# Queries of batch 0 in two token halves, transposed on TensorE, the second half inside the first dense layer

## The chip, the cores and the metric

The kernel runs on one core of one Trainium2 chip. The metric is the device time of one execution in microseconds (us); less is better. The engines are named as in the profile: PE is TensorE's matmul side, PEld its weight load, DVE is VectorE, ACT is ScalarE, POOL is GpSimd and SP is SyncE, which here only issues DMAs.

## The reference

Two layers follow each other. The first is attention within blocks, after a learnt soft sorting of the blocks (4 batches, 8 heads, 768 tokens of 64 elements, 8 blocks of 96 tokens):

```python
P = sort_net                          # (4, 8, 8, 8)
for _ in range(5):
    P = P - np.max(P, axis=-1, keepdims=True)
    P = np.exp(P)
    P = P / (np.sum(P, axis=-1, keepdims=True) + 1e-09)
    P = P / (np.sum(P, axis=-2, keepdims=True) + 1e-09)
k_sorted = np.einsum('bhij,bhjcd->bhicd', P, k_b)      # v likewise
scores = scale * np.matmul(q_b, k_sb.transpose(0, 1, 2, 4, 3))
attn = softmax(scores)
out = np.matmul(attn, v_sb)
```

The second is a dense layer with 3072 tokens, 512 model and 2048 hidden elements:

```python
h = x @ w_in
r = np.maximum(h, 0.0)
g = s * (r * r) + b
return g @ w_out
```

Inputs and output are float32; inside, the kernel works in bfloat16 with float32 sums.

## The kernel before, in words

**Tiling.** A batch has two halves of 384 tokens (TG = 384, four blocks each). A half is one tile of the dense layer; there are eight, t = 0 to 7. The order of all work is written out by hand: every engine runs its instructions in the order of the source, and the lists of "slots" say after which piece of a dense layer a piece of attention of the next batch is issued.

**Opening.** SP loads the sorting logits (L74) and v of batch 0 in four quarters (v0f, L78). POOL loads q and k of batch 0 in three parts each (L112, L113), makes the identity matrix and two helpers (L117 to L124), and in load_w (L129) loads w_in in sixteen pieces and w_out in four. PE runs 30 filler matmuls on zeros (warm, L175). The loop at L176 normalises the sorting matrix five times: one exp on ACT and six or seven small operations on DVE per round. From round 1 on, ACT copies one quarter of v into the layout that sorting needs (permute, L179) behind each exp. 

**Batch 0.** build_pd (L199) turns the matrix into pd, the moving operand that sorts keys and values. qk_piece (L227) multiplies a third of the queries with a 0/1 matrix (qid) or a third of the keys with pd: 32 matmuls of 64 columns into one PSUM tile, then a copy (evac, L219) by ACT ("A") or DVE ("D"). v_piece (L244) does a quarter of the values in the same way. The queries go first (L409 to L411), then two v pieces, three k pieces, two v pieces. s_piece (L257) makes the scores of one pair of heads (hp) for a half: 8 matmuls, one exp on ACT. p_piece (L287) multiplies with the values: 8 matmuls, a reciprocal and a product x on DVE (L303, L304). t_piece (L309) transposes x of two head pairs on PE and copies them to xt. L409 to L435 do this for half 0 and the first two score pieces of half 1.

**Buffers.** PSUM has two pools: psa with three buffers of two banks (all pieces, scores, products and first-layer outputs) and psb with two buffers of one bank (fillers, pd, transposes, second-layer outputs, and the scores of s_banks, L271). A tile waits until the one three (or two) before it in its pool has been read.

**Dense layer.** ffn1 (L348) makes eight pieces per tile: 8 matmuls of 384 columns (L361), ReLU on ACT (L371), square on DVE (gt, L372). With ahead=3, three pieces are begun with half of their matmuls. ffn2 (L376) makes three output rows of blocks with 16 matmuls each (L382), and store (L401) scales, adds the bias and sends out. The call at L504 puts the rest of batch 0's half 1 into the slots of tile 0's first layer: two score pieces by s_banks, four products, two transposes. make_bias (L462) sums w_out's rows for the constant b; POOL copies the result (L474).

**The next batches.** POOL loads v, k and q of batch 1 after w_out (L444), sorts v's layout in eight copies (v_sort, L449, L158), and loads batch 2. Batch 1's queries use qk_piece in slot 4 of tile 0's second layer (L492); for batches 2 and 3 the queries arrive as token rows (load_q_rows) and are transposed by DMA (q_dma, L331). halves (L487) gives the slots of the second layers: s0 for the first tile of a batch, s1 for the second.

## Time and profile before

| | |
|---|---|
| three runs | 235.73, 236.42, 236.75 us, median 236.42 |
| the profiled execution | 233.61 us, span 231.8 us |
| PE busy | 218.9 us of the span, of which fillers (L149) 10.5 |
| granted PE clock, mean | 0.993 |
| POOL's DMA queue | 12.85 MB, 38.4% of 16 engines' time |
| SP's DMA queue | 11.81 MB, 20.8% |
| sorting matrix done / pd ready | 12.01 / 13.85 us |
| first dense matmul | 28.42 us |
| tile 0's first layer done with half 1's attention | 42.29 us |
| first second-layer matmul | 55.17 us |

Durations that come up often (mean of one): first-layer group of 8 matmuls 1.30 us, ReLU 0.81, square 0.56, exp of a score piece 0.81, product x 0.69 and its reciprocal 0.20, eviction of 1024 elements 1.02 on ACT and 1.22 on DVE, 32 sorting matmuls about 0.6, POOL's copy in v_sort 0.89. A view's "idle before" names what ended an engine's wait; the chain of waits follows the work that ended last back to the start, so that each of its pieces is on the path. "issue" is time in which an engine waited for nothing that the profile shows. Times in the timeline count from the start of the span.

### The profile page before, as it was taken

To read this page: it belongs to the slowest core of one execution; us is meant where nothing else is said; L and a number is where in the kernel's file an instruction comes from. 1 tells how busy PE (TensorE), PEld (TensorE's weight loads), DVE (VectorE), ACT (ScalarE), POOL (GpSimd) and SP (SyncE) were. 2 spreads that over 40 slices of the span, in tenths; PEclk is the share of its full clock that TensorE was granted. 3 is DMA by queue.
4 is the path that set the end of the run, shared out by engine and by line. 5 is a ranking of instruction groups with operands and counts; after the bars stand their busy time and mean duration, and the time that the engine had idled before them with its cause. 6 is when DMAs were issued, how large, how long until landed. Compare 5 with 4: busy or idle time off the path is not lost.

```text
span 231.8 us, 5897 instructions
## 1 busy us (share of the span) xinstructions
PE 218.9 (94%) x2584; PEld 129.9 (56%) x2607; DVE 123.7 (53%) x236; ACT 98.3 (42%) x123; POOL 59.4 (26%) x97
## 2 busy tenths in 40 slices
PE   7885899999999999999999999999999999999994
PEld 3464556656555656566455565656455565554453
DVE  6764637499584665445355664446265763432221
ACT  4776764645212345665113435664024446560000
POOL 7538850696581894000000000000000000000000
PEclk9979999999999999999999999999999999999999
DMA  6999999959999958600111299200121452001112
GB/s 151 286 202 171 166 207 218 213 102 206 160 186 223 199 124 138 113 0 3 45 48 48 60 148 164 42 0 3 45 79 63 111 73 45 0 4 45 66 70 92
DMA packets 38826, 25.03 MB, mean 108 GB/s; under 512 B 29328, under 2 KB 33680, under 8 KB 38800
## 3 DMA queue, kind: packets, MB, share of 16 engines
q0 software_dynamic: 18896, 12.85, 38.4%
q1 hardware_dynamic: 19904, 11.81, 20.8%
q8 instruction: 20, 0.33, 0.5%
q14 instruction: 6, 0.05, 0.1%
HBM read 27.27 MB, written 6.29 MB: 145 GB/s over the span
## 4 chain that ended last, share of the span: by engine, by line
PE 87%; DMA 4%; ACT 3%; issue 2%; DVE 2%; SPq 1%
PE hps L361 35%; PE ops L382 34%; PE tv L248 4%; DMA v0f<-in_v_dram 4%; PE tp L236 4%; PE pv L298 3%; PE sc L263 3%; PE ops L395 2%; DVE x L304 1%; ACT rt L371 1%; PE tr L318 1%; ACT vp L156 1%; SPq L78 1%; DVE ks L223 1%; PE pe L201 0%
## 5 line engine op out<-in xcount | busy, mean ns | idle before, releaser
L361 PE MATMUL hps<-xt,wi 128*128 128x384 bf16 x512 | 85.9, 326 | 0.6 <-DVE x L304 0.5
L382 PE MATMUL ops<-wo,gt 128*128 128x512 bf16 x347 | 81.5, 379 | 2.2 <-issue 1.6
L371 ACT ACTIVATE rt<-hps 128x768 bf16<-128x768 f32 x64 | 51.7, 812 | 41.5 <-PE hps L361 38.8
L361 PEld LDWEIGHTS <-wi 128*128 128x128 bf16 x512 | 49.0, 98 | 32.6 <-DVE x L304 0.6
L372 DVE TENSOR_TENSOR gt<-rt 128x768 bf16<-128x768 bf16 x64 | 37.1, 583 | 44.3 <-ACT rt L371 44.2
L382 PEld LDWEIGHTS <-gt 128*128 128x128 bf16 x368 | 33.7, 98 | 37.0
L403 DVE SCALAR_TENSOR_TENSOR ot<-ops,s_bc,bias 128x512 f32<-128x512 f32 (+1 forms) x25 | 18.2, 729 | 37.4 <-PE ops L382 32.6
L268 ACT ACTIVATE at<-sc 112x768 bf16<-112x768 f32 x30 | 22.6, 810 | 31.5 <-PE sc L263 31.5
L304 DVE TENSOR_TENSOR x<-pv,rec 96x512 bf16<-96x512 f32 x32 | 22.0, 687 | 1.1
L158 POOL COPY vp<-rawv 128x384 bf16<-128x384 bf16 x24 | 20.0, 890 | 10.0 <-DMA rawv<-in_v_dram 9.9
L298 PEld LDWEIGHTS <-at 112*128 112x128 bf16 (+1 forms) x256 | 12.7, 101 | 7.5 <-ACT at L268 1.2
L223 DVE CAST vs<-tv 112x1024 bf16<-112x1024 f32 x11 | 13.2, 1221 | 5.9 <-PE tv L248 5.9
L99 POOL DMA_DIRECT2D qtok<-in_q_dram x16 | 12.4, 791 | 10.6 <-DMA rawv<-in_v_dram 7.6
L221 ACT CAST vs<-tv 112x1024 bf16<-112x1024 f32 x5 | 5.1, 1021 | 22.4 <-PE tv L248 22.4
L298 PE MATMUL pv<-vs,at 112*128 112x66 bf16 (+1 forms) x256 | 13.8, 195 | 0.3 <-ACT at L268 0.3
L248 PE MATMUL tv<-pd,vp 128*64 128x64 bf16 x512 | 10.7, 202 | 2.4 <-issue 1.3
L248 PEld LDWEIGHTS <-vp 128*64 128x64 bf16 x512 | 9.8, 118 | 5.6 <-issue 4.6
L303 DVE RECIPROCAL rec<-pv 96x8 f32<-96x8 f32 x32 | 6.4, 200 | 10.8 <-PE pv L298 10.8
L149 PE MATMUL z<-zeros 128*128 128x512 bf16 x37 | 10.5, 420 | 1.6 <-DVE zeros L103 1.2
L134 POOL DMA_DIRECT2D wi<-in_moe_w_in_dram x16 | 8.5, 536 | 6.8 <-DMA rawk<-in_k_dram 3.4
L263 PE MATMUL sc<-qt,ks 64*128 64x96 bf16 x240 | 8.1, 204 | 0.7 <-ACT vs L221 0.7
L223 DVE CAST ks<-tp 128x1024 bf16<-128x1024 f32 x7 | 8.3, 1219 | 0.5 <-PE tp L236 0.3
(69 smaller groups left out, 107.5 us busy)
## 6 DMA issues: line engine op xcount, KB each, us to landing
out_dram<-ot SPq DMA_DIRECT2D x23, 256.0 KB, 2.0
rawv<-in_v_dram POOLq DMA_DIRECT2D x3, 768.0 KB, 12.2
rawk<-in_k_dram POOLq DMA_DIRECT2D x3, 768.0 KB, 7.4
wi<-in_moe_w_in_dram POOLq DMA_DIRECT2D x16, 128.0 KB, 6.6
wo<-in_moe_w_out_dram POOLq DMA_DIRECT2D x4, 512.0 KB, 10.1
v0f<-in_v_dram SPq DMA_DIRECT2D x4, 384.0 KB, 6.6
qtok<-in_q_dram POOLq DMA_DIRECT2D x16, 96.0 KB, 11.2
rawq<-in_q_dram POOLq DMA_DIRECT2D x3, 256.0 KB, 7.0
```

Source lines behind the costliest of these rows:

```text
L158: eng.tensor_copy(out=o, in_=i)
L223: nc.vector.tensor_copy(out=out, in_=in_)
L248: nc.tensor.matmul(out=ps[z * GAP:(z + 1) * GAP, d, :], lhsT=VP[b % 2][:, d0 + d, :], rhs=PD[b][:, :, z, :], start=True, stop=True)
L263: nc.tensor.matmul(out=sc[:, e, n * BLK:(n + 1) * BLK], lhsT=KS[b % 2][pr, g0 + n].rearrange("p z c -> p (z c)"), rhs=q_of(b, pr, hp, half ...
L268: nc.scalar.activation(out=at, in_=sc[0:KR, :, 0:TG], func=AF.Exp, scale=scale)
L298: nc.tensor.matmul(out=pv[0:m, e, n * VW:(n + 1) * VW], lhsT=atf[:, c0:c0 + m], rhs=VS[b % 2][:, e * NG + g0 + n, :], start=True, stop=True)
L304: nc.vector.tensor_tensor(out=x[:, :, hp * 128:(hp + 1) * 128].rearrange("p n (e d) -> p e n d", e=2), in0=pvv[:, :, :, 0:D], in1=rec.unsq ...
L361: nc.tensor.matmul(out=H1[i][:, f, 0:TG], lhsT=wi[:, hp, fc:fc + 128], rhs=xt[:, :, hp, :], start=(hp == 0), stop=(hp == NHP - 1))
L371: nc.scalar.activation(out=rt, in_=h, func=AF.Relu)
L372: nc.vector.tensor_tensor(out=gt[:, 2 * i:2 * i + 2, :], in0=rt, in1=rt, op=ALU.mult)
L382: nc.tensor.matmul(out=ops, lhsT=gt[:, f, m * 128:(m + 1) * 128], rhs=wo[:, f, :], start=(f == 0), stop=(f == NF - 1))
L403: nc.vector.scalar_tensor_tensor(out=ot[:, ns], in0=ops, scalar=s_bc, in1=BIAS[0][:, ns], op0=ALU.mult, op1=ALU.add)
```

## The change

- **Loads.** The identity and emat are made first on POOL. q of batch 0 comes as two halves of 64 partitions (load_qh, six consecutive tokens per partition); POOL's order is: half 0 of q, k in three parts, w_in's first quarter in eight small pieces, its second quarter in four, half 1 of q, the rest of w_in, the two scalars, v of batch 1, w_out. v_sort(1) follows; the loads of k and q of batch 1 and of batch 2 come behind it.
- **Queries.** qid and the query matmuls are gone. q_trans transposes half a batch with 48 PE transposes into one psa tile; q_evac copies it to QT[b], a layout [half, head pair, 6, 64]. Half 0 of batch 0 is transposed before pd, with two ACT copies; half 1 in slot 1 of tile 0's first layer, with one DVE copy. Batch 1 uses the same in the second layers.
- **Scores.** s_piece and s_banks read the queries as 6 runs of 16 and write PSUM in that shape; the exp undoes it while reading.
- **Opening.** A dummy exp ahead of the loop; fillers of 256 columns (44 and 14) and all of one warm call in one PSUM tile; ACT copies a quarter of v in each of rounds 0 to 3 (before: 1 to 4).
- **Order.** Keys before values; the first two score pieces of half 0 by s_banks; the last two v pieces are evicted in token halves, DVE the first and ACT the second; t_piece handles one head pair; first-layer matmuls of pieces 0 and 1 (head pairs 0 and 1) are issued between the attention pieces. All four score pieces of half 1 are in tile 0's first layer.
- **Later.** v of batch 1 is sorted ahead of its keys in the second layer of tile 0 (slots 5, 7, 9, 11); pd of batches 2 and 3 is built in the first layers of tiles 2 and 4.

```diff
+    def load_qh(b, half):
+        if b not in QH:
+            QH[b] = rawp.tile([128, H, CQ, D], BF, tag="rawq", name="qh")
+        qv = q[b].rearrange("h (f p c) d -> f p h (c d)", f=2, c=CQ)
+        nc.gpsimd.dma_start(out=QH[b][half * 64:(half + 1) * 64].rearrange("p h c d -> p h (c d)"),
+                            in_=qv[half])
...
-    load("q", 0, 3)
-    load("k", 0, 3)
...
+    load_qh(0, 0)
+    load("k", 0, 3)
+    fill_vs(0)
...
+    for u in range(2):
+        for c in range(2):
+            for a in range(2):
+                load_wi(c * W8, (c + 1) * W8, slice(2 * u + a, 2 * u + a + 1))
+    for a in range(NHP):
+        load_wi(W4, 2 * W4, slice(a, a + 1))
+    load_qh(0, 1)
+    for c in range(2, 4):
+        for a in range(NHP):
+            load_wi(c * W4, (c + 1) * W4, slice(a, a + 1))
...
+    load("v", 1)
...
+    def q_trans(b, half):
...
+        tr = psa.tile([128, 2, 1024], BF, tag="a", name="tqa")
+        pr = slice(half * 64, (half + 1) * 64)
+        for a in range(NHP):
+            for c in range(CQ):
+                for e in range(2):
+                    o = (a % 2 * CQ + c) * 64
+                    nc.tensor.transpose(out=tr[e * 64:(e + 1) * 64, a // 2, o:o + 64],
+                                        in_=QH[b][pr, 2 * a + e, c, :], identity=ident[pr, pr])
+        return tr
+
+    def q_evac(b, half, us, eng, tr):
+        evac(eng, QT[b][:, half].rearrange("p (u a) c t -> p u (a c t)", u=2)[:, us],
+             tr[:, us, 0:2 * TG])
...
-    warm(30)
+    warm(44, 256)
     for it in range(5):
         nc.scalar.activation(out=sn, in_=sn, func=AF.Exp)
-        if it >= 1:
-            permute(nc.scalar, 0, v0f, slice((it - 1) * CV, it * CV))
-        if it == 2:
-            load_w()
+        if it < 4:
+            permute(nc.scalar, 0, v0f, slice(it * CV, (it + 1) * CV))
...
+    tq = q_trans(0, 0)
+    for u in range(2):
+        q_evac(0, 0, slice(u, u + 1), "A", tq)
+    warm(14, 256)
...
+                if byp:
+                    o = sc[:, e, 0:TG].rearrange("p (c t) -> p c t", c=CQ)[:, :, 16 * n:16 * n + 16]
+                    r = QT[b][pr, half, hp, :, 16 * n:16 * n + 16]
...
+        if byp:
+            nc.scalar.activation(out=at.rearrange("p e (t c) -> p e t c", c=CQ),
+                                 in_=sc[0:KR, :, 0:TG].rearrange("p e (c t) -> p e t c", c=CQ),
+                                 func=AF.Exp, scale=scale)
...
-    qk_piece("q", 0, 0, "A")
-    qk_piece("q", 0, CK, "A")
-    qk_piece("q", 0, 2 * CK, "D", first=lambda: build_pd(0))
+    build_pd(0)
     warm(3)
-    v_piece(0, 0, "A")
-    v_piece(0, CK, "D")
-    qk_piece("k", 0, 0, "A")
-    qk_piece("k", 0, CK, "D")
-    qk_piece("k", 0, 2 * CK, "A")
-    v_piece(0, 2 * CK, "D")
-    v_piece(0, 3 * CK, "A")
-    s_piece(0, 0, 0)
...
+    k_piece(0, 0, "A")
+    k_piece(0, CK, "D")
+    k_piece(0, 2 * CK, "A")
+    v_piece(0, 0, "D")
+    v_piece(0, CK, "A")
+    s_banks(0, 0, 0)
+    v2 = v_piece(0, 2 * CK, "D", 1)
+    v3 = v_piece(0, 3 * CK, "D", 1)
+    v2("A")
+    s_banks(0, 0, 1)
+    v3("A")
     warm(1)
     p_piece(0, 0, 0)
+    s_piece(0, 0, 2)
+    warm(1)
     p_piece(0, 0, 1)
+    t_piece(0, 0, 0, "A")
+    s_piece(0, 0, 3)
+    part(0, 0, (0,))
+    t_piece(0, 0, 1, "A")
     p_piece(0, 0, 2)
+    part(0, 0, (1,))
+    t_piece(0, 0, 2, "A")
     p_piece(0, 0, 3)
+    part(0, 1, (0, 1))
+    t_piece(0, 0, 3, "D")
...
-    ffn1(0, {0: [SB(2)], 1: [P(0, 1, 0)], 2: [SB(3)], 3: [P(0, 1, 1)], 4: [P(0, 1, 2)],
-             5: [P(0, 1, 3)], 6: [TP(0, 1, 0, "A")], 7: [TP(0, 1, 2, "D")]}, ahead=3)
-    ffn1(1, {1: [PDB(1)], 3: [PDB(2)], 4: [make_bias], 6: [PDB(3)]}, ahead=3)
+    ffn1(0, {1: [QF0()], 2: [SC(0, 1, 0)], 3: [SC(0, 1, 1)], 4: [P(0, 1, 0), SC(0, 1, 2)],
+             5: [P(0, 1, 1), TP(0, 1, 0, "A"), SC(0, 1, 3)],
+             6: [P(0, 1, 2), TP(0, 1, 1, "D")], 7: [P(0, 1, 3), TP(0, 1, 2, "A")]},
+         {0: 2, 1: 2})
+    v_sort(1)
+    part(1, 0, (0, 1))
+    t_piece(0, 1, 3, "D")
+    part(1, 1, (0, 1))
+    load1()
+    load2()
+    ffn1(1, {2: [PDB(1)], 5: [make_bias]}, {0: 2, 1: 2})
```

## The prediction

> **What bounds the kernel now.** I read the page from its top: engine table, slices, chain; then the timeline of the first 50 us.

> ```profile
> PE 218.9 (94%) x2584; PEld 129.9 (56%) x2607; DVE 123.7 (53%) x236; ACT 98.3 (42%) x123; POOL 59.4 (26%) x97
> ...
> PE   7885899999999999999999999999999999999994
> ...
> PEclk9979999999999999999999999999999999999999
> ```

> PE is full from the sixth slice (29 us) on. Only in the first five can time be won; what is added to PE later is paid in full, unless it fills a hole. The chain of waits tells what the opening waits for:

> ```profile
> 2.62 9.28 DMA v0f<-in_v_dram
> 11.90 0.02 issue
> 11.92 1.50 ACT vp L156
> 13.43 0.92 ACT qt L221
> 14.34 0.04 issue
> 14.38 1.98 PE tv L248 x64
> ...
> 19.81 1.34 issue
> 21.16 0.28 PE tv L248 x5
> ...
> 28.59 2.62 PE hps L361 x16
> ```

> The last quarter of v of batch 0 lands at 11.90; ScalarE rearranges it, evicts queries, and PE starts. The sorting matrix (pd, L213) is ready at 13.85 by the timeline; the first dense layer starts at 28.42. The windows give two disturbances in between: PE's granted clock is 0.50 from 15 to 17 us, and PE stands 1.34 us in the middle of one piece, where no instruction waits on another engine.

> Let P be the time when pd of batch 0 is ready, S the time from which the first dense layer can run through, E the time when tile 0's layer and the attention of tile 1 are done (42.29 before).

> **1. P moves from 13.85 to 14.5: +0.65.** Before, exp and rearranging copy are interleaved as exp0, exp1, copy0, exp2, copy1...; after, as exp0, copy0, exp1, copy1... ScalarE is in order, so the last exp now stands behind copy3, that is behind the last quarter of v. The quarters landed at 4.6, 7.4, 9.6 and 11.9 (issue plus 3.4 to 9.3 us). They should come earlier: POOL now makes ident and emat first (0.27 + 0.29 + 0.52 + 0.85 us in the trace, with gaps 2.1), so its first transfer is issued at 3.4, not 1.26, and SP's four have the DMA engines alone until about 4.7. In the first 14 us the SP queue moved 1.58 MB for 35.0% of the engines' time, 322 GB/s when alone; shared, it had about half. Alone from 3.0 to 4.7 gives 0.65 MB with the start-up; the other 0.92 MB takes 2.85 us alone, 5.4 shared: the quarters land at about 4.0, 5.5, 7.8, 10.1. A copy is 1.5, an exp 0.26, VectorE from exp to exp 1.48: copy0 4.0-5.5, exp1 5.55, copy1 to 7.35, exp2 7.4, copy2 to 9.35, exp3 9.4, copy3 10.2-11.7, exp4 11.75-12.0, matrix done 12.65 (12.01 before), P 1.84 later as before: 14.5. Bounds: if ScalarE never waits for v after 3.4, nine operations end at 10.7 and P is 13.25 (-0.6); if the quarters land as before, P is 16.2 (+2.35).

> **2. From P to S: 14.57 becomes 13.25, -1.3.** The queries' 96 matmuls and three evictions leave the front; 48 transposes (as small as L236's: 96 in 1.71, so 0.85) run at about 10 us, their two ScalarE copies (0.80 each, as xt<-tr) end about 14.1, under the wait for pd. Then the order is k, k, k, v, v, scores, v, v. With 0.6 per piece on PE, ScalarE eviction 1.02, VectorE 1.23, halves 0.6, two-bank exp 0.43 each, scores 0.35, and three buffers of pool psa: k evictions end P+1.7, 2.5, 2.8; v0 P+3.75, v1 P+4.2; first exps P+5.1; half evictions for token half 0 P+5.4; second exps P+6.5; first attention product P+6.35 (it waits for a filler that needs a bank); then per head pair 0.93 on VectorE, transposes 0.18, copies 0.43: the last xt arrives at P+12.45. The same walk through the kernel before gives 13.25 without its two disturbances, 14.57 with them, so I trust it to some tenths. Disturbances stay:

> ```profile
> PE 87%; DMA 4%; ACT 3%; issue 2%; DVE 2%; SPq 1%
> ...
> q8 instruction: 20, 0.33, 0.5%
> ```

> PE's 5191 instructions came in 20 packets of a queue of their own, some 260 each. Counted in PE's program order, the 1.34 us gap is at instruction 698, a second (0.49 at 62.69) at 1711, 1013 or nearly four packets further: PE ran out of instructions. Instruction 442, one packet earlier, ran at about 16.7, so the packet came 4.5 us later. In the new order instruction 442 is in v0 (P+2.1) and 698 in the second score group (P+5.45): the packet comes at P+6.6, and S is P+12.95. [...] For the clock I add 0.3 (half of some 0.6, since PE waits before pd as it did). Bounds: 12.45 (neither) and 14.4 (a packet in 6 us, as between 57.2 and 63.17, and the full clock loss).

> **3. Work carried over S: 0.** At S the new kernel has nine first-layer matmuls done (9 x 0.163 = 1.47) but still owes 48 transposes (0.85) and two score pieces (0.6).

> **4. The first layer of tile 0: +1.7 of waits, +0.4 of slower VectorE.** Before, three pieces were started ahead and PE idled 0.6 of 13.87. Now psa's three buffers also serve transposed queries, scores and products, in program order. Walk: ReLU 0.81, exp 0.81, gt 0.56, reciprocal and x 0.93, piece 1.30. The query copy on VectorE (1536 elements, twice xt's 0.56: 1.1) stands behind gt of piece 1 and ends S+3.9, PE would score at S+3.3: 0.6. Later pieces wait 0.2 (ReLU 4), 0.25 (x of pair 0), 0.1, 0.25 (x of pair 2), and the last transposes 0.9: x of pair 3 stands behind the gt of piece 7 on VectorE. Sum 2.3, less the 0.6 of before. And POOL's sort of v(1) moves into this stage: v(1) is now asked for ahead of wo, 4.46 MB into POOL's transfers, at 0.19 MB/us (windows 12 to 21 us) landed by about 31, sorted 31 to 38. What such a neighbour costs VectorE shows where it ran before (42.4 to 49.75):

> ```profile
> 42.99 0.69 DVE L372 TENSOR_TENSOR gt<-rt 128x768 bf16<-128x768 bf16 x1 [1.08 <-ACT rt L371]
> ...
> 45.93 2.32 DVE L372 TENSOR_TENSOR gt<-rt 128x768 bf16<-128x768 bf16 x2 [1.79 <-ACT rt L371]
> ```

> gt took 0.91 on average there against 0.56, and nobody waited for it; now x and the transposes stand behind it. Five fall under the sort, 0.35 each, 1.75, of which a quarter lies on the path: 0.4. [...] Bounds for all of 4: 0 (buffers turn round as before) and +3.5 (waits of 2.3 plus all 1.75).

> **5. Later: +0.1.** Batch 1's queries: 96 matmuls and three evictions become 96 transposes and two copies, equal on PE. K, V and Q of batch 1 now stand closer together in the second layer of tile 0 (some 700 PE instructions in 11.6 us, 4.2 per packet against 4.5 to 6 to fetch): +0.3 beside the old 0.49. The bias copies stood behind query loads that waited for DMA until 60.32, and VectorE waited 2.5 for them; POOL's next loads now follow the sort at 38, while wo still moves, where the queue ran dry before (102 GB/s in one slice): -0.2. pd of batches 2 and 3 only moves. Bounds -0.5 and +1.

> Edits at nothing: the dummy exp (the table load ended at 2.03, exp0 waits for VectorE until 2.81); SP's order is unchanged; on POOL every transfer waits for the eighth before it, as wi waited for rawq and rawk, and the weights still come in time: by P+9 = 23.5 POOL's queue has moved about 0.55 MB shared and 2.5 alone, the first layer's first pieces need 1.7. The second query half lands by about 21, is needed at 28.6. wo ends by about 42, the bias matmuls read it at about 49. Were that cover gone, PE would wait for the difference. Matmuls with rows of 16 strided elements and PSUM output of that shape are not in the trace: below, 0.043 each as L263's; above, twice that, 96 of them in the full part, +4.1. PE reads xt with gaps between its rows at 0.163 per 384 columns, the nearest row: I take 0. ScalarE's strided PSUM reads cost 1.0 ns per element in ks<-tp, as plain ones.

> **Sum:** 0.65 - 1.3 + 0 + 2.1 + 0.1 = +1.55. The profiled execution took 233.61 (span 231.8 and 1.8 around it), so 235.2; it ran below the runs shown (median 236.42), and on their scale it is **238.0**, 0.7% slower. About 0.5%, 1.2 us, is what a measurement of this kernel can tell from no change.

> **Rivals.**
> - *PE is fed in the first layer (faster).* If buffers and VectorE keep up, the waits of 4 fall to 0.5, the packet comes in time (S = P+12.45, -2.1), and P is 14.2: 0.35 - 2.1 + 0.5 = -1.25 to -2.0 with P earlier, so about 234.8. For it: ScalarE has only 10.5 us of work in a stage of 15, VectorE 9.9. Against: program order puts x behind gt. It decides when the waits of 4 are under 0.5.
> - *No change.* Only v lands early (P 13.4): 1.55 - 1.1 = +0.45, 236.9.
> - *v lands as late as before (slower still).* Half of q and k on POOL's queue still take their share, P is 16.2: 1.55 + 1.7 = +3.25, 239.7. For it: 9.28 us on the chain before. Against: POOL's 2 us later start.

> **How the numbers follow.** Forecast 0.40 (0.30 slower, 0.10 within 0.5%), fed PE 0.25, no change 0.15, late v 0.20. So faster 0.25, same 0.25, slower 0.50. The range goes from 233.5 (P -0.6, S -2.1, 4 at +0.3, later -0.5: -2.9) to 240.9 (late v, and a further 1.2 from the upper bounds of 2 and 4); strided matmuls at double cost are left out, with under 0.1. The forecast's own range is 237 to 239.2.

> **What would show it.** Step 1: landing of the last v quarter and the last exp near 10.1 and 11.75, pd near 14.5. Step 2: first hps at P+8.5 to 9, a mid-piece "issue" gap in the second score group. Step 4: hps and pv waiting on ACT and DVE between 28 and 45, 2 us or more, gt above 0.8 while POOL copies v. I am wrong if pd comes before 13.9, if PE idles under 0.8 in that stage, or if scores take over 0.5 per piece.

## The result, and the profile after

The changed kernel takes 245.66 us (median of four runs, 244.11 to 246.31), the kernel before beside it 236.18 (235.73 to 236.75): a ratio of 1.039, 95% interval 1.034 to 1.045. The forecast was 238.0 with a range up to 240.9. Ratios below leave out runs over 1.5% above the fastest of their own kernel; medians keep them.

The profiled execution took 244.11, its span 242.3 against 231.8 before, 10.5 more. By the medians it is 9.5 more: the traced execution of the kernel before took 233.61 and is faster than the four runs beside the result. On the page of the changed kernel PE's slices have holes in the second to the fifth and at the sixteenth, and the granted clock dips in the third, the fifth and the sixth:

```profile
PE 223.8 (92%) x2608; PEld 134.3 (55%) x2631; DVE 124.3 (51%) x236; ACT 100.6 (41%) x129; POOL 62.6 (26%) x99
...
PE   8487699989999997999999999999999999999994
...
PEclk9979659999999999999999999999999999999999
```

The timeline of its PE shows where the opening goes (start, length, line, operation; idle time before it in brackets):

```profile
11.70 1.05 PE L209 MATMUL tqa<-ident,qh 64*64 64x64 bf16 x48 [3.41 <-DMA qh<-in_q_dram]
12.68 3.17 PE L129 MATMUL z<-zeros 128*128 128x256 bf16 x14
15.78 0.43 PE L255 MATMUL pe<-sn,emat 32*128 32x64 f32 x2
16.14 0.82 PE L129 MATMUL z<-zeros 128*128 128x512 bf16 x2
17.56 1.71 PE L280 MATMUL tp<-pd,rawk 128*64 128x64 bf16 x96 [0.60 <-DVE pd L267]
...
22.64 0.33 PE L340 MATMUL scb<-qt,ks 64*128 64x96 bf16 x7 [0.18 <-ACT at L345]
26.04 0.61 PE L129 MATMUL z<-zeros 128*128 128x512 bf16 x1 [3.07 <-issue]
```

The sorting matrix is done at 12.24, so v is no longer what it waits for. But the matmul that begins pd (L255) runs only at 15.78: it stands behind the transposes, which wait 3.41 for the first query half, and behind 14 fillers. Then PE stands 3.07 us, to 26.04, waiting for nothing that the profile shows, with a DMA share of 1.18. Both traces have 20 packets in a queue of instructions (q8, 0.33 MB); one of them moved at 23.7 us, 2.3 before PE went on, and in the kernel before one at 18.8, 2.3 before its gap ended at 21.16. So the gap is read here as a wait for instructions. The windows (busy time by engine, then the granted clock, DMA share and GB/s) show what follows:

```profile
24.00:27.00 3.00, 0.96 (x9) 0.66 (x9) 0.00 (x0) 0.34 (x1) 1.07 (x2) 0.84 1.15 170
27.00:30.00 3.00, 2.87 (x33) 1.85 (x32) 1.78 (x4) 1.90 (x3) 2.50 (x4) 0.50 1.27 180
30.00:33.00 3.00, 2.78 (x28) 1.90 (x27) 0.89 (x2) 1.05 (x3) 2.96 (x6) 0.50 0.85 138
33.00:36.00 3.00, 2.87 (x14) 1.25 (x12) 1.25 (x3) 0.06 (x1) 1.08 (x4) 0.50 1.03 194
```

PE is nearly full from 27 to 36 us and works at half its clock, in the dense layer. Later, one wait that the kernel before did not have, and POOL's share in it:

```profile
96.48 0.82 PE L409 MATMUL hps<-xt,wi 128*128 128x384 bf16 x4 [1.61 <-DMA xt<-x]
```

```profile
76.75 0.56 POOL L93 DMA_DIRECT2D rawk<-in_k_dram  x1 [9.71 <-PE tp L280]
```

The keys of batch 1 are now sorted late in the second layer of tile 0. POOL's load of batch 3's keys needs their buffer and waits for that, so it and the loads behind it (to 90 us) move beside the DMA transpose of x, which takes 7.1 us at a DMA share of 1.79, where before it took 4.2 at 0.65 (81 to 86 us).

The checkpoints, by stage (us of the profiled executions):

| stage | before | forecast | after |
|---|---|---|---|
| pd ready | 13.85 | 14.5 | 17.5 |
| from there until the first layer runs through (S) | 14.57 | 13.25 | 17.5 |
| S to the end of that stage (E, at 42.29 before) | 13.87 | 15.97 | 17.05 |
| E to the first second-layer matmul | 12.88 | | 11.70 |
| to the first layer of tile 2 | 31.62 | | 32.73 |
| from there to the end | 145.0 | | 145.8 |

The differences are +3.65, +2.9, +3.2, -1.2, +1.1 and +0.8: 10.5. E after is the start of the last transposes, 52.05; the dense matmuls behind them start at 52.23.

### The profile page after: what moved, and what is told of

The parts are those of the page before. It is cut to its first block, busy times and chain, and to the rows that moved or that the text cites. A ratio compares the mean times of both kernels' runs of the same rounds, so it can differ in the third digit from the quotient of the medians.

```text
span 242.3 us, 5949 instructions
## 1 busy us (share of the span) xinstructions
PE 223.8 (92%) x2608; PEld 134.3 (55%) x2631; DVE 124.3 (51%) x236; ACT 100.6 (41%) x129; POOL 62.6 (26%) x99
## 4 chain that ended last, share of the span: by engine, by line
PE 83%; DMA 7%; ACT 4%; DVE 3%; issue 2%; POOL 1%; POOLq 0%
PE hps L409 34%; PE ops L433 31%; DMA qh<-in_q_dram 4%; PE tv L290 3%; PE pv L361 3%; DMA xt<-x 3%; PE sc L322 2%; PE tp L280 2%; PE z L129 2%; ACT rt L421 2%; PE ops L446 1%; PE tqa L209 1%; PE tr L378 1%; ACT vs L196 1%; DVE gt L422 1%
## 5 line engine op out<-in xcount | busy, mean ns | idle before, releaser
L409 PE MATMUL hps<-xt,wi 128*128 128x384 bf16 x512 | 88.6, 331 | 2.5 <-DMA xt<-x 1.6
L421 ACT ACTIVATE rt<-hps 128x768 bf16<-128x768 f32 x64 | 51.7, 811 | 46.3 <-PE hps L409 44.2
L422 DVE TENSOR_TENSOR gt<-rt 128x768 bf16<-128x768 bf16 x64 | 40.7, 639 | 43.9 <-ACT rt L421 43.4
L454 DVE SCALAR_TENSOR_TENSOR ot<-ops,s_bc,bias 128x512 f32<-128x512 f32 (+1 forms) x25 | 18.2, 730 | 36.3 <-PE ops L433 32.7
L361 PEld LDWEIGHTS <-at 112*128 112x128 bf16 (+1 forms) x256 | 13.9, 106 | 7.0 <-ACT at L330 0.6
L129 PE MATMUL z<-zeros 128*128 128x256 bf16 (+1 forms) x62 | 12.2, 367 | 4.3 <-issue 3.1
L196 ACT CAST vs<-tv 112x1024 bf16<-112x1024 f32 (+1 forms) x7 | 6.3, 899 | 23.2 <-PE tv L290 23.2
L326 ACT ACTIVATE at<-sc 112x768 bf16<-112x768 f32 x14 | 10.9, 809 | 10.6 <-PE sc L322 10.5
L361 PE MATMUL pv<-vs,at 112*128 112x66 bf16 (+1 forms) x256 | 14.8, 202 | 0.0
L198 DVE CAST vs<-tv 112x1024 bf16<-112x1024 f32 (+1 forms) x11 | 12.1, 1124 | 5.0 <-PE tv L290 4.9
L139 POOL DMA_DIRECT2D wi<-in_moe_w_in_dram x20 | 10.7, 552 | 8.6 <-DMA qh<-in_q_dram 5.8
L129 PEld LDWEIGHTS <-zeros 128*128 128x128 bf16 x63 | 7.6, 125 | 7.1 <-issue 3.2
L290 PEld LDWEIGHTS <-vp 128*64 128x64 bf16 x512 | 8.9, 113 | 3.0 <-issue 2.7
```

Source lines behind the costliest of these rows:

```text
L129: nc.tensor.matmul(out=z[0:m, 0:w], lhsT=zeros[:, 0:m], rhs=zeros[:, 0:w], start=True, stop=True)
L198: nc.vector.tensor_copy(out=out, in_=in_)
L290: nc.tensor.matmul(out=ps[z * GAP:(z + 1) * GAP, d, :], lhsT=VP[b % 2][:, d0 + d, :], rhs=PD[b][:, :, z, :], start=True, stop=True)
L361: nc.tensor.matmul(out=pv[0:m, e, n * VW:(n + 1) * VW], lhsT=atf[:, c0:c0 + m], rhs=VS[b % 2][:, e * NG + g0 + n, :], start=True, stop=True)
L409: nc.tensor.matmul(out=H1[t, i][:, f, 0:TG], lhsT=wi[:, hp, fc:fc + 128], rhs=XT[t][:, :, hp, :], start=(hp == 0), stop=(hp == NHP - 1))
L421: nc.scalar.activation(out=rt, in_=h, func=AF.Relu)
```

## The experiments

All are edits of the changed kernel unless another is named, compared with the kernel before on the same chip. Theory at the start: PE's order ahead of pd and the packets of instructions carry the loss. Rivals: the first layer's buffers; fillers that the clock needs.

**e1_no14.** Without the fillers behind the transposes:

```diff
-    warm(14, 256)
```

> Edit: the 14 fillers between the query transposes and the pd matmul are left out. Theory A (PE's program order holds pd back: it stands behind the first query half, landed at 11.65, and 14 fillers that took 3.1 us at half clock; and PE's instructions come in packets of some 256 that take 4.5 to 6.4 us): pd ready near 14.6 instead of 17.5; but the packet that begins at instruction 442 is then late too, so a gap of 1 to 2.7 us in the middle of the first v piece; first attention product near 23.5 instead of 26.4; the whole 2 to 3 us faster than the changed kernel. Theory B (the loss is in the first dense layer, in buffers and VectorE, and the front is hidden): under 0.7 us faster. Theory C (the fillers keep the clock up): slower, with the clock at 0.5 for longer after pd.

240.15 (239.38 to 240.8), ratio 1.011 (1.008 to 1.015). pd comes at 14.61:

```profile
12.88 0.43 PE L254 MATMUL pe<-sn,emat 32*128 32x64 f32 x2
...
14.66 2.51 PE L279 MATMUL tp<-pd,rawk 128*64 128x64 bf16 x96
```

No long packet gap appears in this trace, the clock is 1.0 from 17 to 60 us, and the second layers start at 56.69 instead of 63.75. Of these 7.1 us, 3.3 are left at the end (240.80 against 244.11 for the two profiled executions): VectorE's first output waits 6.80 for the bias copies on POOL, and the two second layers take 36.5 instead of 32.7. Nor are all 7.1 due to the fillers: e5 and e7 below have the same PE order up to there, had the gap again, and their second layers start at 62.00 and 59.19. Most of the loss lies ahead of the first layer, and a second loss had been hidden behind the first.

**e2_front512.** Wider fillers at the start:

```diff
-    warm(44, 256)
+    warm(44, 512)
```

> Edit: the 44 opening fillers have 512 columns instead of 256, so PE is busy until the queries land; the number of instructions is the same. If the idle 3.4 us before the transposes lowers the clock: granted clock 1.0 from 12 to 15 us, the 14 fillers take 1.5 instead of 3.1, pd at about 16.0 instead of 17.5. Theory A with packets: the packet from instruction 442 is asked for at about 12.8, so a gap of about 1 us appears in the first v piece, the packet from 698 is no earlier than 25, and the whole gains at most 1 us. Without packets: the whole gains 1.5 and the 3.1 us gap ahead of the first attention product stays or goes with what it waits for.

242.97 (242.91 to 246.23), ratio 1.028 (1.020 to 1.035). The clock stays at 1.0 from 9 to 27 us, but the fillers end at 13.56, and the pd matmul runs at 15.99 all the same. The gap (2.81 at 26.00) and the half clock behind it (27 to 34) stay: a warm start did not prevent them.

**e3_packet.** As long, but 29 matmuls fewer ahead of the same work, 58 PE instructions with their weight loads:

```diff
-    warm(44, 256)
+    warm(22, 512)
...
-    warm(14, 256)
+    warm(7, 512)
```

> Edit: 22 and 7 fillers of 512 columns in place of 44 and 14 of 256: the same PE time, 58 instructions fewer. Theory A (gaps sit at fixed instruction numbers near 442 and 698, whatever stands there): the 3.1 us gap ahead of the filler before the first product is gone from there; a gap of 2 to 4 us appears in the middle of the second v piece (instruction 442), and a second, smaller one in the first transpose of x (698). The whole within 1.5 us of the changed kernel. Rival (the gap is a wait for a PSUM bank or for ScalarE): it stays ahead of that filler, about 3 us.

242.98 (240.8 to 245.27), ratio 1.020 (1.014 to 1.027). PE's timeline shows the gap at another instruction:

```profile
18.59 1.10 PE L290 MATMUL tv<-pd,vp 128*64 128x64 bf16 x45
23.05 0.74 PE L290 MATMUL tv<-pd,vp 128*64 128x64 bf16 x19 [3.35 <-issue]
```

It stands inside the second piece of v, after 45 of 64 matmuls. Counted from the traces, 445 PE instructions (matmuls and weight loads) stand ahead of it, and 701 ahead of the gap in the kernel before, the changed kernel, e2 and e4: 256 apart. So it belongs to the count, not to the operation there. The second, smaller gap that was expected at some 698 did not come.

**e4_korder.** Batch 1's keys back to the first slot of the second layer:

```diff
-            s0 = {5: [V(n, 0, "D"), V(n, 1, "A")], 7: [V(n, 2, "D"), V(n, 3, "A")],
-                  9: [K(n, 0, "D"), K(n, 1, "A"), K(n, 2, "D")], 11: [QF(n, 0, "A")]}
+            s0 = {0: [K(n, 0, "D"), K(n, 1, "A"), K(n, 2, "D")], 4: [QF(n, 0, "A"), QF(n, 1, "D")],
+                  8: [V(n, 0, "D"), V(n, 1, "A"), V(n, 2, "D")]}
...
-        s1 = {0: [QF(n, 1, "D") if n == 1 else V(n, 3, "D"), SC(n, 0, 0), SC(n, 0, 1)],
+        s1 = {0: [V(n, 3, "D"), SC(n, 0, 0), SC(n, 0, 1)],
```

> Edit: in tile 0's second layer the old order of batch 1 comes back: keys in slot 0, both query halves in slot 4, values from slot 8, the last v piece in the next tile. Theory A: POOL's load of keys of batch 3 no longer waits 9.7 us for the keys of batch 1, the loads end before the DMA transposes of x, the first transpose lands in about 4 instead of 7.1 us, and PE's 1.6 us wait at tile 2's first layer goes: 1.5 to 2 us faster than the changed kernel. Rival (the transpose is late because everything before it is): the wait stays, the whole within 0.6 us.

240.11 (239.46 to 244.78), ratio 1.010 (1.007 to 1.013). The wait for x is gone. But the opening, left as it was, differs too: the query half landed at 11.18, the 14 fillers took 1.70 at full clock, and the half clock behind a gap of 2.77 lasted 3.4 us. Three runs are near 240 and one at 244.78, so a run of the unaltered kernel was needed.

**c0_again.** No edit.

> The changed kernel once more, unaltered. The kernel with the key order put back ran at 239.5 to 240.4 with a mean clock of 0.986 to 0.993 and at 244.8 with 0.965, though nothing of it was altered between its runs. Theory K (a part of the slowdown is the granted clock after the packet gap, and it differs from run to run): the times spread over 3 us or more, each 0.01 of mean clock goes with some 1.8 us, and the fast ones are at 241 to 242 (the 1.7 us of the late transposed x of tile 2 stay). Rival (the changed kernel is always at 244 to 246): all runs within 2 us of 245 whatever the clock.

243.88 (239.98 to 247.38, six runs), ratio 1.022 (1.015 to 1.028). By mean clock: 0.986: 239.98; 0.979: 243.06; 0.978: 242.69; 0.972: 244.69; 0.964: 245.46 and 247.38. That is some 2.8 us per 0.01 of clock, steeper than expected (1.8). In the traces the half clock comes in stretches of 3.41 us or multiples of that (3.41 and 10.24 in the changed kernel's, 6.83 twice in this one's); one such stretch is 0.007 of this kernel's mean clock, so by estimate these runs had two to five of them, at some 2.0 us each. The kernel before spread over 3.0 us in 14 runs. So a part of the loss is a dip that differs from run to run, and it is not the whole: even the fastest run is 3 us over before's median (236.88).

**e5_both.** e1 and e4 together.

> Without the 14 fillers and with the keys of batch 1 in their old place. Theory A (the two losses are independent): 240.1 less the 1.7 us wait for the transposed x of tile 2 = 238.4, and the third tile's first layer starts with no wait. Rival (tile 2 is late for another reason, the second layer of tiles 0 and 1, 36.5 us where the kernel before took 31.6): that layer is still some 36 long, the wait for x was hidden under it in part, and the time is 239.5 to 240.

239.99 (235.64 to 241.01, seven runs), ratio 1.003 (0.997 to 1.009); by the medians it is 1.013. The profiled run, at 241.01, has a gap of 2.42 with 10 us of half clock behind it:

```profile
25.66 0.34 PE L321 MATMUL sc<-qt,ks 64*128 64x96 bf16 x4 [2.42 <-issue]
```

Tile 2 waits no more, and the second layers take 31.4. Unclear by itself: the runs scatter by more than the question.

**e6_pdfirst.** e5, with the sorting matrix ahead of the queries:

```diff
-    tq = q_trans(0, 0)
-    for u in range(2):
-        q_evac(0, 0, slice(u, u + 1), "A", tq)
...
     build_pd(0)
+    tq = q_trans(0, 0)
+    for u in range(2):
+        q_evac(0, 0, slice(u, u + 1), "A", tq)
     warm(3)
```

> As the last one, and the matmul of the sorting matrix ahead of the transposes of the queries in PE's order, so that neither the query's landing nor a filler stands ahead of it. Theory A (PE's order ahead of that matmul made pd late): pd is ready 1.84 after the matrix, at 14.1 instead of 14.6, the transposes run under its VectorE chain, and the time is 0.5 below the last one. Rival (the clock, low after the wait for the queries, and the evictions set the pace of the keys): pd earlier, first attention product at the same time, and no difference.

240.1 (239.05 to 241.03), ratio 1.014 (1.009 to 1.018): no gain. PE's timeline says why:

```profile
12.41 0.66 PE L251 MATMUL pe<-sn,emat 32*128 32x64 f32 x2 [4.76 <-DVE sn L236]
12.99 1.49 PE L209 MATMUL tqa<-ident,qh 64*64 64x64 bf16 x48
```

The matmul is in time now, but PE had stood 4.76 us, the clock is 0.5 from 11 to 18, and the transposes take 1.49 instead of 0.95. The rival was right on this edit: the first attention product starts at 22.72, in e5 at 22.61. With the fillers too short, the clock is low ahead of it (e11 has it at 21.70 at full clock).

**e7_load2.** e5, with the loads of batch 2 behind the second first layer:

```diff
     load1()
-    load2()
     ffn1(1, {2: [PDB(1)], 5: [make_bias]}, {0: 2, 1: 2})
+    load2()
```

> As the one without fillers and with the old key order, and the loads of batch 2 asked for after the bias is made, so that POOL's three copies of the bias do not stand behind DMA requests that wait for a place. Theory D (the second layer of tiles 0 and 1 starts earlier than the bias is ready, and waits for it on POOL): the copies run at some 53 to 56, the two second layers take 31.6 to 32.5 instead of 36.5, and the time is 4 us lower, 234.5. Rival (the second layer is long because the clock is low in it): still 36, no gain.

243.97 (242.34 to 245.1), ratio 1.030 (1.025 to 1.035). Half right: the wait for the bias copies is gone, from the second layer's start at 59.19 to tile 2 are 31.75 us of work, and then PE stands 3.92 for x, whose DMA transpose took 9.4 beside the loads that were moved there. Moving all of them gave it back.

**e8_quiet.** e5, with a lull in POOL's loads:

```diff
+    hold = const.tile([128, 1024], BF)
+    for _ in range(9):
+        nc.gpsimd.memset(hold, 0.0)
     for a in range(NHP):
         load_wi(W4, 2 * W4, slice(a, a + 1))
     load_qh(0, 1)
```

> As the kernel without fillers and with the old key order, and nine fillings of a scratch tile (some 8.7 us) on POOL ahead of the second quarter of the first layer's weights, so that the DMA queues run empty between some 20 and 25 us, while PE's packet of instructions is under way. Theory F (the packet comes 4.4 to 6.4 us after it is asked for because it shares the DMA engines with the loads): it comes in under 3 us, the gap of 2.4 us at instruction 698 is gone or under 0.3, the clock stays at 1.0 from 24 to 36 us, and the time is 235 to 236. Rival (the fetch takes that long by itself): the gap stays at 2 us or more and so does the half clock, and the time is 239 to 241.

245.59 (243.04 to 247.62), ratio 1.034 (1.026 to 1.042). The packet gap is gone: the DMA share is 0.05 from 18 to 21 us and 0.01 to 24 us, and PE has no issue gap over 0.22 us there. The expected time failed because the lull held back the second query half too: PE stood 3.65 for it at 34.63, again with half clock around it. It held back the bias copies as well: VectorE's first output waited 8.30 for them, and PE 2.50 for VectorE.

**e9_pause4 and e10_pause0.** The kernel *before*, with a pause in pure dense work, pause(4) in e9 and pause(0) in e10:

```diff
+    pz = const.tile([128, 512], BF)
+
+    def pause(n):
+        z = psb.tile([128, 512], FP, tag="b", name="z")
+        nc.tensor.matmul(out=z, lhsT=zeros[:, 0:128], rhs=zeros, start=True, stop=True)
+        nc.scalar.copy(out=pz, in_=z)
+        for _ in range(n):
+            nc.scalar.copy(out=pz, in_=pz)
+        z = psb.tile([128, 512], FP, tag="b", name="z")
+        nc.tensor.matmul(out=z, lhsT=zeros[:, 0:128], rhs=pz, start=True, stop=True)
...
         ffn1(2 * b, {})
+        if b == B - 1:
+            pause(4)
         ffn1(2 * b + 1, {})
```

> The kernel before the change, with PE made to wait between the two first layers of the last batch (some 200 us), where nothing else bounds it: one more matmul of zeros, five ScalarE copies of 512 columns in a chain behind it, and a matmul that reads the last. Nothing else is changed. Theory K (PE's granted clock falls after a pause of some 3 us): PE stands 3.5 to 4 us, then the clock is 0.5 for 3 to 10 us, and the time is 5 to 9 us over before. Rival (the clock dips in the opening have another cause, such as the DMA traffic, and a pause costs its own length): the clock stays at 1.0 and the time is 3.5 to 4 us over before.

> The same with one copy in place of five, a pause of 1.2 to 1.5 us, as long as the packet gap of the kernel before. Theory K: too short to move the clock; the time is 1.2 to 1.6 over before. Rival (any pause is followed by the half clock): 3 us or more over before, clock 0.5 for some us behind it.

PE's timeline of e9: the same 64 matmuls of a first layer ahead of the pause and behind it.

```profile
189.41 10.57 PE L361 MATMUL hps<-xt,wi 128*128 128x384 bf16 x64
203.95 0.38 PE L511 MATMUL z<-pz,zeros 128*128 128x512 bf16 x1 [3.97 <-ACT pz L509]
204.17 12.24 PE L361 MATMUL hps<-xt,wi 128*128 128x384 bf16 x64
```

And its windows behind the pause, with no DMA at all (the last two columns):

```profile
204.00:207.40 3.40, 3.40 (x12) 1.66 (x12) 0.00 (x0) 0.55 (x1) 0.00 (x0) 0.54 0.00 0
207.40:211.00 3.60, 3.60 (x23) 2.11 (x22) 1.33 (x3) 1.89 (x3) 0.00 (x0) 0.96 0.00 0
```

The pause costs its 3.97 and 1.67 more for the clock, 5.6 in all; the runs say 242.27 (241.85 to 243.81) against 236.67, 5.6. In e10 the pause is 1.38, the 64 matmuls behind it take 10.56, the clock stays at 1.0, and the runs say 238.32 (237.69 to 239.9), 1.65. So a pause can make the dip by itself; with a DMA share of 0.00 the traffic was not needed for it.

**e11_fill, e12_hold5, e13_hold3.** e6 with this; e11 without the hunk of load_qh and hold, e12 with five fillings:

```diff
+    load_qh(0, 1)
+    hold = const.tile([128, 1024], BF)
+    for _ in range(3):
+        nc.gpsimd.memset(hold, 0.0)
     for a in range(NHP):
         load_wi(W4, 2 * W4, slice(a, a + 1))
-    load_qh(0, 1)
...
-    warm(44, 256)
+    warm(38)
...
-        load_q_rows(2)
...
     ffn1(1, {2: [PDB(1)], 5: [make_bias]}, {0: 2, 1: 2})
+    load_q_rows(2)
```

> From the kernel with the sorting matrix's matmul first, no 14 fillers and the old key order: 38 fillers of 512 columns in place of 44 of 256, so that PE works until some 12.2 us, and the row loads of batch 2's queries asked for behind the first layers, so that the bias copies on POOL don't stand behind them. Theory K with packets: no pause and no dip ahead of pd, keys from 14.2 at the full clock; the packet gap of 2 to 3 us at instruction 698 stays, with 3 to 10 us of half clock behind it in most runs: 237 to 241, the runs spread. Rival (the dips follow the DMA traffic and not the pauses): the half clock at 12 to 18 stays, no gain over 240.

> The same, with the second half of the queries asked for ahead of the second quarter of weights and five fillings of a scratch tile (5 us) on POOL behind it, so that the DMA queues run dry while PE fetches its packet. Theory (pauses and what follows them are the whole loss over the forecast): no PE pause over 1 us up to 50 us, clock 1.0 all through, first second-layer matmul at 55.5 to 56.5 (55.2 before), 234 to 236.5, and the spread of the runs under 2 us. Rival (the change itself loses, by the waits in the first layer): without pauses still 238 or more, first second-layer matmul past 58.

> The same with three fillings (3 us). If the lull of 3 us at 18 to 21 still covers the fetch, as the last one; if the loads are back before the packet has come, a gap of 1 to 2.5 us at instruction 698 and 236 to 240.

| kernel | median (runs) | ratio | packet gap | first second-layer matmul |
|---|---|---|---|---|
| e11 | 238.02 (235.84 to 239.94) | 1.002 (0.998 to 1.006) | 1.02 and 2.08 | 59.70 |
| e12 | 236.69 (235.8 to 237.15) | 0.998 (0.995 to 1.001) | none | 55.76 |
| e13 | 234.95 (234.92 to 235.65) | 0.990 (0.986 to 0.994) | 0.31 | 55.75 |

e13's page and PE timeline:

```profile
PE   7988799799999999999999999999999999999994
...
PEclk9999999999999999999999999999999999999999
```

```profile
12.51 0.40 PE L254 MATMUL pe<-sn,emat 32*128 32x64 f32 x2 [0.50 <-DVE sn L239]
12.84 0.94 PE L212 MATMUL tqa<-ident,qh 64*64 64x64 bf16 x48
13.71 0.82 PE L129 MATMUL z<-zeros 128*128 128x512 bf16 x3
14.47 1.71 PE L279 MATMUL tp<-pd,rawk 128*64 128x64 bf16 x96
...
17.52 0.64 PE L289 MATMUL tv<-pd,vp 128*64 128x64 bf16 x29 [0.31 <-issue]
```

With the long pauses and the dips away, e13 is 1% below the runs of the kernel before beside it (median 237.11, 235.43 to 238.04), and its four runs lie within 0.7 us. That it is the faster kernel is not shown. The traced execution of the kernel before took 233.61, three of its seven runs beside e17 took 233.76 to 234.24, and that trace is ahead of e13's at the second layers (55.17 against 55.75) and at tile 2 (86.79 against 87.26). Besides, e13 is the change with several further edits. e12's profiled run has a dip at 14 to 18 us and a gap of 1.91 later, in its second layer.

**e15_after_hold.** The changed kernel with that hunk alone, and seven fillings:

```diff
+    load_qh(0, 1)
+    hold = const.tile([128, 1024], BF)
+    for _ in range(7):
+        nc.gpsimd.memset(hold, 0.0)
...
-    load_qh(0, 1)
```

> The changed kernel with the second half of the queries asked for ahead of the second quarter of weights and seven fillings (7 us) on POOL behind it; nothing else is altered. Theory K (the packet gap and the half clock behind it cost the changed kernel some 6 to 7 of its 7 to 9 us... less what the late matrix costs, 3): gap gone, clock 1.0 from 18 to 40 us, 239 to 240.5, and the runs no further than 2 us apart. Rival (the gap only stands beside waits that are there anyway): under 2 us gained, 242 or more.

246.78 (244.69 to 247.57), ratio 1.039 (1.033 to 1.046): the rival's number, but not for its reason. The gap is gone and the second layers begin 6.3 us earlier (57.43), although a wait of 1.13 for ScalarE still left 6.8 us of half clock at 23 to 30. All of it is lost at once behind that. POOL, VectorE and PE:

```profile
68.95 0.77 POOL L113 DMA_DIRECT2D qtok<-in_q_dram  x1 [3.49 <-DMA rawv<-in_v_dram]
69.76 1.90 POOL L528 COPY bias<-bias 32x512 f32<-32x512 f32 x3
```

```profile
71.70 0.75 DVE L457 SCALAR_TENSOR_TENSOR ot<-ops,s_bc,bias 128x512 f32<-128x512 f32 x1 [12.30 <-POOL bias L528]
```

```profile
73.63 1.07 PE L293 MATMUL tv<-pd,vp 128*64 128x64 bf16 x32 [7.27 <-DVE vs L201]
```

The bias copies stand in POOL's order behind row loads of queries, the last of which waits 3.49 for a load of v to land; VectorE's first output waits 12.30 for them, v's evictions stand behind it, and PE stands 7.27. The lull itself makes this worse, since POOL's later work moves with it: the copies end at 71.7, in e1 without a lull at 65.2. In the changed kernel they end at 67.0, and the late opening covers this.

**e17_hold_rows.** e15, with e4's edit and this:

```diff
-        load_q_rows(2)
...
     ffn1(1, {2: [PDB(1)], 5: [make_bias]}, {0: 2, 1: 2})
+    load_q_rows(2)
```

> The changed kernel with the lull of 7 us, the keys of batch 1 in their old place and the row loads of batch 2's queries behind the first layers; the fillers and PE's order ahead of pd are the change's. Theory (late matrix, packet gap, bias copies and late x are the whole loss): first second-layer matmul at 57 to 58, the two second layers 31.5 to 32.5, first layer of tile 2 at 89 to 90, and 237 to 239. Rival (something else in the second layers loses too): 35 us or more there, 241 or more.

238.89 (237.45 to 240.19), ratio 1.018 (1.008 to 1.028). Second layers from 56.33 (expected 57 to 58), tile 2 at 89.82; the two layers take 33.5 with two packet gaps (0.49, 1.11) and 0.71 for x, over the 32.5 expected. Its PE program is e4's, instruction by instruction, so the two show the packet with and without loads beside it. e4, then e17:

```profile
17.26 1.42 PE L290 MATMUL tv<-pd,vp 128*64 128x64 bf16 x64
...
23.64 0.39 PE L129 MATMUL z<-zeros 128*128 128x512 bf16 x1 [2.77 <-issue]
```

```profile
17.03 1.42 PE L293 MATMUL tv<-pd,vp 128*64 128x64 bf16 x64
...
21.31 0.39 PE L129 MATMUL z<-zeros 128*128 128x512 bf16 x1 [0.66 <-ACT at L348]
```

If a packet is asked for 256 instructions ahead (an estimate from the distance that e3 shows: the 15th of these 64 matmuls, so 17.6 and 17.4), it took 6.0 us in e4, with a DMA share of 0.87 to 1.19, and at most 3.9 in e17, where the filler waits for ScalarE alone and the DMA share falls from 1.2 to 0.0 on the way.

**e14_before_hold and e16_before_hold11.** Does the kernel *before* gain by a lull? Five fillings in e14, eleven in e16:

```diff
+        hold = const.tile([128, 1024], BF)
         for c in range(4):
+            if c == 1:
+                for _ in range(5):
+                    nc.gpsimd.memset(hold, 0.0)
```

> The kernel before the change, with five fillings of a scratch tile on POOL (5 us) behind the first quarter of the weights, so that its packet is fetched while the DMA queues are empty. Theory M (part of the 1% comes from the lull): the gap of 1.3 to 2.6 us at 21 us goes, and the time is 1 to 2 us lower, 235 to 236. Rival (the gap of the kernel before stands beside other waits, and the whole 1% is the change's): the time stays within 0.5% of before, 236.5 to 237.5.

> The kernel before, with eleven fillings (11 us, to 20.6 us) behind the first quarter of the weights in place of five. Theory M (the lull is worth something there too): no packet gap at 21 us, 1 to 2 us less, 235 to 236. Rival (the gap of the kernel before costs nothing, because evictions on ScalarE and VectorE set the pace there): within 0.5% of before.

Neither tells. In e14 (237.5, ratio 0.998, 0.990 to 1.006) the DMA share was 1.19 to 1.27 from 16 to 20 us, and the gap stayed at 1.86, with one of 0.74 ahead of it. In e16 (244.0, ratio 1.038, 1.029 to 1.048) memsets of POOL that batch 0's first attention product needs (vs, L148) had moved behind the lull with the loads, and PE stood 6.79 for them. Its gap stayed too, at 1.04, although the DMA share was 0.03 and less from 18 us on:

```profile
20.58 0.26 PE L252 MATMUL tv<-pd,vp 128*64 128x64 bf16 x5 [1.04 <-issue]
```

By the same count that packet took 3.7 us (16.85 to 20.58). So by this estimate the packet took less time under a lull (3.7, at most 3.9 in e17) than under loads (6.0 in e4), and a gap could still be left. What a clean lull is worth to the kernel before is open.

## Why the prediction was wrong

The direction was right and the size was not. Of the 8.9 us between the forecast (+1.55) and the two traces (+10.5), 3.0 are step 1's, 4.2 step 2's, 1.1 step 4's and 0.6 step 5's.

**Step 1 failed.** It took pd as the matrix plus 1.84 of VectorE work. Its first half held (matrix at 12.24, forecast 12.65, since v came early). The second left out PE's order: it had the transposes "at about 10 us", and did not count the 14 fillers at all. The query half took 8.99 us to land, the fillers 3.17 at a low clock (0.50 from 13 to 15 us), and pd came at 17.5: 3.0 over the forecast. The runs show the other side: without the fillers pd is ready at 14.61 (e1), with its matmul first and no pause ahead at 14.2 (e13). The low clock has a large share: in e4, e15 and e17, with the same PE order up to there, the half landed at 10.7 to 11.2, no dip followed, and pd came at 14.9 to 15.4; in c0's trace, with a dip, at 17.5 again.

**Step 2 failed in size.** Its gap stood where it said, at the second score group, but was 3.07 and not the 1.15 that its own 4.5 us for a packet gave: by the same count, an estimate, the packet took 6.3 us. And the author's estimate for the clock was 0.3, for a wait ahead of pd; the dip of 10.2 us *behind* the gap, on a full PE, was not in it. The longer gap is 1.9 of the 4.2; the other 2.3 fall into the 9 us of half clock ahead of S. e9 measures the link by itself, e13 shows both gone. In seven kernels with the change (itself, e2 to e6 and e11) PE stood 2.07 to 3.46 us in such a gap.

**Step 4 held in its waits.** From S to E PE stood 17.05 - 14.79 = 2.26 us (forecast 2.3), for the query copy 0.60, ReLUs 0.35 and 0.18, and x 0.32 and 0.75. The 0.4 more for VectorE beside POOL did not show as a wait, though the squares were as slow as it took them to be: the four under POOL's sort (36.5 to 44.2) took 0.89 on average, 1.08 at the worst, against 0.91 forecast. It can be worse: under POOL's next sort, near 99 us, one square took 4.03, but PE did not wait for it. Scores over strided rows cost 0.34 for eight at full clock, nothing more, as taken. The stage is 1.1 longer than forecast: its waits are 0.4 shorter, and its work is 1.5 longer, of which half clock until 36.3 is 0.6 and four matmuls of tile 1 that now stand ahead of E are 0.65.

**Step 5 failed twice.** It gave -0.2 for the bias copies; in fact eight row loads of queries stand ahead of them on POOL as before. As soon as the opening is not late they cost something: VectorE waits 6.80 and PE 1.78 in e1, and PE 7.27 in e15, where the lull adds to it. And it did not see that keys sorted later hold POOL's next loads back until they meet x's transposes (1.6, gone in e4). The stage from E on is 1.2 shorter because work left it: two of the sorting matrices (0.36 each) went to later tiles, and the four matmuls (0.65) were done ahead of E.

**The rivals.** Late v is refuted, by the matrix at 12.24. PE fed in the first layer did not come about: e13, at 234.95, has its time (234.8), but by luck: PE stands 2.2 us there too. What decided was in none of the cases: an order on PE, and pauses with half clock behind them.

## What to carry to other kernels

When is a result ready? Walk the order of the engine that makes it, fillers and instructions that wait for a DMA included, not only the chain of its data. In this opening, with its bursts of small matmuls beside loads, PE stood up to 3.46 us (c0) and waited for nothing that the profile shows; a lull of 3 us in the loads, with one needed load moved ahead of it, was worth 3 us here by the medians (e11 against e13); with a lull of 5 us it was 1.3 (e12). And when a stage is made earlier, look at what the next one waits for on the queue that nobody had to wait for yet.
